# Sliding-window attention into a squared-ReLU MoE layer: first V loaded by token halves, products with V in pairs, column sums spread by copies, and a plan with other costs

## The chip, the core and the metric

One core of one Trainium2 chip. The kernel is a program for five instruction streams (TensorE, ScalarE, VectorE, GpSimd, SyncE; in the profile PE, ACT, DVE, POOL and SP). The metric is the time of one execution on the device in microseconds. A profile is one further execution, recorded instruction by instruction; its span runs from the first to the last instruction.

## What is computed

q, k and v are [8 batches, 8 heads, 576 tokens, 64] in float32. Each token attends to the tokens at most 32 places away; the result, 4608 tokens of 512 numbers, goes through two matrices with a squared ReLU between them.

```python
scores = scale * np.matmul(q, k.transpose(0, 1, 3, 2))
mask = np.abs(pos[:, None] - pos[None, :]) <= window      # window = 32
attn = softmax(np.where(mask, scores, -1e9))
x = (attn @ v).transpose(0, 2, 1, 3).reshape(B * S, H * D)  # [4608, 512]
r = np.maximum(x @ w_in, 0.0)                              # w_in [512, 2048]
out = (s * (r * r) + b) @ w_out                            # w_out [2048, 512]
```

Since `b` is one number, `b @ w_out` is `b` times the column sums of w_out. The kernel computes `s * ((r * r) @ w_out) + b * colsum`.

## The kernel before

**Tasks and a plan.** The kernel writes no instruction directly. It adds tasks to a graph with `add` (L95): a stream, one or more instructions, an estimated cost in ns, the resources that it reads and writes, and a key (a due time; the smaller goes first). `plan` (L126) simulates the streams and the DMA queue with these costs, and each time takes the task that can start first, by key where several can. `emit` (L234) writes each stream in the planned order, with semaphore waits for what comes from other streams. So each engine's order is fixed when the kernel is built; an engine whose next instruction waits stands still, whatever lies behind it. The order of tasks in the program sets who reads and writes a buffer before whom. SP's loads have keys below -100 and go in program order.

**Batches.** Batches 0 and 1 are treated by pairs of heads (`load_pair`, `turn_pair`, `pair_scores`): k and q of a pair are loaded (256 KB each, 512 tokens), cast to bf16 (L691), transposed on PE (L704), copied out (L709 for q on ACT, L710 for k on DVE), multiplied (L943) and put through the exponential (L986). The last 64 tokens come separately (`load_rest`, `turn_rest`, `last_scores`). The products with V are made in units of 128 tokens, five to a batch (`av_part`, L868): half of the 64-row products, a wait, then the other half; then `finish` takes the reciprocal of the row sums (L892), multiplies (L894, DVE), transposes (L901, PE) and copies into XT (L909, ACT). XT is the input of the MoE layer. Later batches go through DMA transposes and `unit`, in which a unit's products with V share a task with the next unit's scores, which then lie between the two halves.

**V of batch 0.** `load_rows` (L595) loads 512 tokens in two DMAs, four heads each; partition p holds tokens 4p to 4p+3, all 128 partitions. One cast for each half of the heads goes to VN (L602). `place_v` (L613) brings the tokens into the right partitions by products with a shifted identity (L620, 24 of them), and the results are copied from PSUM into VB (L629, L630). The last 64 tokens come by `load_tail` and `place_tail`.

**The MoE layer.** `s1` makes one block's hidden values: products with w_in (L1123), ReLU (L1130, ACT), square (L1132, DVE). `s2` multiplies 128 tokens by w_out (L1141) and `put` writes them out (L1157, DVE, then a DMA). The first 512 tokens are cut into blocks of 224, 128 and 160; their products with w_out are made by `early` (L1172) two rows of 128 of w_out at a time as these arrive, into four PSUM banks (both halves of O and of AVN). The first block needs units 0 and 1 of batch 0. `FIRST` lists the order in which the quarters of w_in are used by the three blocks; an entry with `None` lets the attention of batch 1 go one step on.

**Weights.** `load_weights` (L542) loads w_in and w_out in 16 pieces of 512 KB through eight staging buffers and casts each (L556, all on POOL). SP's order after the pairs of batch 0 is `ORDER0`: the two row loads of V, the rest of q and k, the tail of V, then the four quarters of w_in. Then comes `ORDER1`: pairs of batch 1, w_out, V and rest of batch 1.

**Column sums.** `colsum` (L1180) sums w_out by 64 products with ones in 32-column groups (L1182), copies four blocks to a block diagonal (L1186), spreads them over all partitions by one float32 product (L1189) and multiplies by b into CVEC (L1191), which `put` adds.

Of the kernel before, what the change touches and what calls it, by code (L numbers as in the profile page):

```python
# [25 lines left out]
K0 = ("dve", "dve", "dve", "dve")  # L26
Q0 = ("act", "pool", "pool", "pool")
RUN = 4
ORDER0 = (("r", 0), ("r", 1), ("e", 0), ("v", 0), ("w", 0), ("w", 1), ("w", 2), ("w", 3))
ROWE = ("pool", "dve")  # L30
WINE = ("pool", "pool", "pool", "pool")
TURNKEY = -17.5
TURN = (None, 0)
FIRST = ((0, 0), (0, 1), (1, 0), (1, 1), (2, 0), (0, 2), (2, 1), (1, 2), (2, 2), (0, 3), (1, 3), (2, 3), TURN, TURN, TURN, TURN)
WOUTE = (("pool", "pool"),) * 4
TAIL = ("act", "dve")
HOST = (("k", 3), ("q", 0))
HELD = (2200.0, 1500.0, 1500.0, 1500.0)
OPEN = -24.4
REST = ("pool", "pool")  # L40
ORDER1 = (("p", 0), ("p", 1), ("w", 0), ("w", 1), ("p", 2), ("p", 3), ("w", 2), ("w", 3), ("v", 0), ("v", 1), ("e", 0), ("v", 2), ("v", 3), ("v", 4))
SWITCH = 215.0
XTS = 4000.0
# [7 lines left out]
SLACK = (1000.0, 2000.0, 3000.0, 3000.0)  # L51
PACEV = ((-1,-1,0,0,1),(0,0,1,1,2),(0,0,1,1,2))
EV0 = ("dve", "act", "dve", "act", "dve")
BANK1 = ("SC", "W", "SC", "AVN", "AVN")
EV1 = ("pool", "pool", "pool", "pool", "pool")
EV2 = ("dve",) * 5
# [3 lines left out]
TURN_DVE = ()  # L60
# [5 lines left out]
class _Task:  # L66
    __slots__ = ("n", "stream", "fns", "cost", "lat", "key", "deps", "users", "left",
                 "ready", "start", "fin", "dma", "sem", "seq", "val", "used", "snap", "slack", "after", "next", "half", "mark")

    def __init__(self, n, stream, fns, cost, lat, key, dma, slack, after):  # L70
# [10 lines left out]
class _Graph:  # L81
# [4 lines left out]
    LAT = {"pe": 260.0, "act": 130.0, "dve": 110.0, "pool": 150.0, "sp": 60.0}  # L86
    MARGIN = 250.0
# [7 lines left out]
    def add(self, stream, fns, cost, reads=(), writes=(), key=0.0, accum=False, dma=None, waits=(),  # L95
            lat=None, slack=0.0):
# [3 lines left out]
        t = _Task(len(self.tasks), stream, fns, cost, self.LAT[stream] if lat is None else lat, key,  # L100
                  dma, slack, after)
# [4 lines left out]
        for r in reads:  # L106
            assert r in self.writer, r
            t.deps.add(self.writer[r])
        for w in writes:
# [16 lines left out]
    def plan(self):  # L126

        free = {s: 600.0 for s in self.STREAMS}
# [7 lines left out]
        order = []  # L136
        rings, clock, room = {"sp": [], "act": []}, [0.0], {}
# [37 lines left out]
        def release(t):  # L175
            for u in t.users:
                u.left -= 1
                if u.stream == "pe" and t.stream == "pe":
                    r = t.fin
                elif t.dma is not None:  # L180
                    r = t.fin + 100.0 + u.slack
                elif u.stream == t.stream:
                    r = t.fin + 60.0
                else:
                    r = t.fin + t.lat + (self.MARGIN if u.stream == "pe" else 0.0)
# [4 lines left out]
        while len(order) < len(self.tasks):  # L190
# [19 lines left out]
            t.start = st  # L210
            free[t.stream] = t.fin = st + t.cost
# [114 lines left out]
def bass_sliding_window_symmetric__then__act_starrelu_kernel(  # L326
# [23 lines left out]
    with ExitStack() as es:  # L350
# [146 lines left out]
        even, block = OUTS[NOUT - 2][:, 0:128], OUTS[NOUT - 1][:, :]  # L497
        done = [g.tasks[-1]]
        add("pool", lambda e: e.memset(even, 1.0 / 32), 150, writes=[("OUTS", NOUT - 2)], key=-95.0, waits=done)
        add("pool", lambda e: e.memset(block, 0.0), 500, writes=[("OUTS", NOUT - 1)], key=-95.0, waits=done)  # L500
# [41 lines left out]
        def load_weights(which, i, x, key, eng):  # L542
# [6 lines left out]
            else:  # L549
# [7 lines left out]
                {"act": 1040.0, "dve": 690.0, "pool": 1100.0}[eng], reads=[("STG", si)], writes=[("W" + which, i, x)],  # L557
                key=key + 150.0, slack=100.0, lat=HELD[i] if which == "out" else None)

# [643 lines left out]
        for m, i in FIRST:  # L1203
# [3 lines left out]
            for ft in range(4 * i, 4 * i + 4, group(m)):  # L1207
                s1(m, ft)
# [265 lines left out]
```

## Time and profile before

| | us |
|---|---|
| median of 3 runs (313.73 to 314.08) | 313.94 |
| span of the profiled execution | 310.6 |
| DVE busy, of the span | 191.8 |
| POOL busy, of the span | 106.8 |
| first product with V (L868) | starts at 14.80 |
| first MoE product (L1123) | starts at 20.20 |
| last piece of w_out cast (L556) | 43.39 to 44.43 |
| first MoE product of the fourth block | starts at 60.00 |
| DMA traffic | 56.09 MB in 100,054 packets |

The page gives busy time, share of the span and number of instructions for each engine; busy time of PE is modelled from the starts of its products. Its second part cuts the span into 40 slices of 7.8 us; a digit is the busy share in tenths. The chain of waits is followed back from the last instruction to whatever released it. A line of the order of time gives start, duration, engine, line, operation, output<-inputs, shapes and count, and in brackets how long the engine had been idle and what ended that.

### The profile page before, as it was taken

What the parts mean: (1) busy time and instruction counts of PE and PEld (TensorE: products, weight loads), DVE (VectorE), ACT (ScalarE), POOL (GpSimd) and SP (SyncE); (2) the same over time, 40 slices, a digit from 0 to 9 for tenths busy, and PEclk for the clock granted to TensorE, in tenths of its full rate; (3) what the DMA queues carried; (4) which work ended last, traced back from release to release, by engine and by line L of the source; (5) the groups of instructions that cost most, each with busy time, mean ns of one, the idle gap of its engine ahead of it and who ended that gap; (6) DMA issues with size and microseconds to landing.
All of it is one profiled execution on the core that took longest, in us unless ns stands there. A gap on an engine that the chain in (4) does not pass through costs nothing.

```text
span 310.6 us, 7883 instructions
## 1 busy us (share of the span) xinstructions
PE 295.3 (95%) x3305; PEld 160.3 (52%) x3348; DVE 191.8 (62%) x372; ACT 142.3 (46%) x224; POOL 106.8 (34%) x125
## 2 busy tenths in 40 slices
PE   7789999999999999999999999999999999999996
PEld 3469754577654454454444444444444444444444
DVE  4675587776677796886379658866655543333312
ACT  4757445256536673763156326635444333333300
POOL 6364786752526366261435331615000000000000
PEclk9999999999999999999999999999999999999999
DMA  7999999998997998899799799978211111000122
GB/s 223 333 384 372 371 268 235 245 168 271 247 192 210 282 184 192 287 145 154 215 291 151 139 262 281 141 146 203 80 53 53 51 46 36 34 34 35 37 96 77
DMA packets 100054, 56.09 MB, mean 181 GB/s; under 512 B 72048, under 2 KB 91248, under 8 KB 100016
## 3 DMA queue, kind: packets, MB, share of 16 engines
q1 hardware_dynamic: 100016, 55.56, 75.3%
q8 instruction: 27, 0.44, 0.6%
q14 instruction: 11, 0.09, 0.1%
HBM read 36.70 MB, written 9.44 MB: 149 GB/s over the span
## 4 chain that ended last, share of the span: by engine, by line
PE 78%; DMA 12%; SPq 3%; issue 2%; POOL 2%; DVE 2%; ACT 0%; POOLq 0%
PE o L1141 35%; PE w L1123 32%; DMA stg<-in_moe_w_out_dram 5%; PE avn L868 4%; DMA stg<-in_moe_w_in_dram 3%; DMA stg<-in_k_dram 3%; PE sc L810 2%; PE avn L1172 2%; DMA stg<-in_v_dram 1%; DVE gt L1132 1%; SPq L666 1%; PE o L1172 1%; POOL wout L556 1%; SPq L677 1%; PE avn L901 1%
## 5 line engine op out<-in xcount | busy, mean ns | idle before, releaser
L1123 PE MATMUL w<-xt,win 128*128 128x512 bf16 (+4 forms) x750 | 138.2, 325 | 2.9 <-ACT r L1130 1.6
L1130 ACT ACTIVATE r<-w 128x512 bf16<-128x512 f32 (+2 forms) x148 | 86.7, 586 | 100.1 <-PE w L1123 84.9
L1132 DVE TENSOR_TENSOR gt<-r 128x512 bf16<-128x512 bf16 (+2 forms) x148 | 87.1, 601 | 69.2 <-ACT r L1130 68.5
L1141 PE MATMUL o<-wout,gt 128*128 128x512 bf16 (+1 forms) x508 | 120.6, 372 | 2.4 <-issue 1.6
L1123 PEld LDWEIGHTS w<-xt,win 128*128 128x128 bf16 x768 | 68.1, 98 | 52.9 <-ACT r L1130 1.2
L1141 PEld LDWEIGHTS o<-wout,gt 128*128 128x128 bf16 x528 | 50.5, 98 | 55.1 <-DVE gt L1132 0.7
L759 POOL CAST nat<-stg 128x1024 bf16<-128x1024 f32 (+1 forms) x36 | 41.1, 1140 | 51.2 <-DMA stg<-in_q_dram 38.2
L776 POOL COPY kt<-ktr 128x512 bf16<-128x512 bf16 (+1 forms) x30 | 30.8, 1028 | 36.0 <-DMA ktr<-nat 34.5
L838 ACT ACTIVATE ex<-sc 128x1024 bf16<-128x1024 f32 (+1 forms) x28 | 28.7, 1023 | 24.4 <-PE avn L868 23.3
L1157 DVE SCALAR_TENSOR_TENSOR outs<-o,sb,cvec 128x512 f32<-128x512 f32 (+1 forms) x35 | 25.5, 732 | 18.9 <-PE o L1141 18.7
L894 DVE TENSOR_TENSOR xn<-avn,rec 128x512 bf16<-128x512 f32 (+1 forms) x31 | 21.4, 690 | 0.9
L842 DVE TENSOR_TENSOR ex<-ex,mask 128x1024 bf16<-128x1024 bf16 (+1 forms) x28 | 19.8, 708 | 1.2 <-ACT ex L838 0.5
L868 PE MATMUL avn<-vb,ex 64*64 64x65 bf16 x944 | 19.9, 197 | 0.3
L868 PEld LDWEIGHTS avn<-vb,ex 64*64 64x64 bf16 x944 | 12.9, 106 | 13.2 <-issue 5.5
L590 DVE CAST vb<-vst 128x512 bf16<-128x512 f32 (+1 forms) x28 | 12.3, 445 | 1.1 <-DMA vst<-in_v_dram 1.1
L892 DVE RECIPROCAL rec<-avn 128x8 f32<-128x8 f32 (+1 forms) x31 | 6.3, 202 | 8.7 <-PE avn L868 8.7
L810 PE MATMUL sc<-qt,kt 64*64 64x128 bf16 x432 | 11.3, 216 | 0.0
L909 ACT COPY xt<-avn 128x512 bf16<-128x512 bf16 (+2 forms) x14 | 7.1, 517 | 9.0 <-PE avn L901 9.0
L556 POOL CAST wout<-stg 128x1024 bf16<-128x1024 f32 x8 | 8.7, 1087 | 5.9 <-DMA stg<-in_moe_w_out_dram 5.7
L556 POOL CAST win<-stg 128x1024 bf16<-128x1024 f32 x8 | 8.4, 1055 | 3.3 <-DMA stg<-in_moe_w_in_dram 3.2
L1172 PE MATMUL o<-wout,gt 128*128 128x512 bf16 x28 | 8.2, 379 | 0.7 <-POOL wout L556 0.5
L986 ACT ACTIVATE ex<-sc 128x1024 bf16<-128x1024 f32 (+2 forms) x7 | 6.2, 902 | 5.0 <-PE sc L943 5.0
(118 smaller groups left out, 140.5 us busy)
## 6 DMA issues: line engine op xcount, KB each, us to landing
out_dram<-outs SPq DMA_DIRECT2D x35, 256.0 KB, 2.5
vst<-in_v_dram SPq DMA_DIRECT2D x28, 256.0 KB, 6.1
stg<-in_k_dram SPq DMA_DIRECT2D x6, 1024.0 KB, 10.4
stg<-in_q_dram SPq DMA_DIRECT2D x6, 1024.0 KB, 5.8
stg<-in_moe_w_in_dram SPq DMA_DIRECT2D x8, 512.0 KB, 8.8
stg<-in_moe_w_out_dram SPq DMA_DIRECT2D x8, 512.0 KB, 7.2
stg<-in_q_dram SPq DMA_DIRECT2D x8, 256.0 KB, 5.2
stg<-in_k_dram SPq DMA_DIRECT2D x8, 256.0 KB, 5.4
```

Of the source, the lines that this page charges most:

```text
L556: add(eng, (lambda e: e.copy(dst, stg)) if eng == "act" else (lambda e: e.tensor_copy(dst, stg)), {"act": 1040.0, "dve": 690.0, "pool": 11 ...
L759: add(eng, lambda e, x=x: e.tensor_copy(nat[0:top, 1024 * x:1024 * x + 1024].rearrange("p (i h d) -> p h i d", h=H, i=2), stg[0:top, :].re ...
L776: add("pool", lambda e, c=c, w=w: e.tensor_copy(KT[slot][:, :, c:c + w].rearrange("p a (s i) -> p a s i", i=4), KTR[slot][:, :, :, c // 4: ...
L838: add("act", lambda e, dst=flat_dst, src=flat_src: e.activation(dst, src, AF.Exp, bias=0.0, scale=0.125), 190 + 0.833 * 512 * len(hs), rea ...
L842: add("dve", lambda e, flat=flat, mask=mask: e.tensor_tensor(flat, flat, mask, ALU.mult), 130 + 0.53 * 512 * len(hs), reads=[("E", ei, hp, ...
L868: return [lambda e: e.matmul(av[64 * x:64 * x + 64, h, 0:D + 1], lhsT=buf[64 * g:64 * g + 64, h % 2, h // 2, c:c + 64], rhs=VB[64 * g:64 * ...
L894: add("dve", lambda e: e.tensor_tensor(XN[xi][0:p1, :].rearrange("p (a c) -> p a c", a=H), av[0:p1, :, 0:D], REC[ri][0:p1, :].rearrange("p ...
L1123: add("pe", [lambda e, g=g, kc=kc: e.matmul(wt[:, g, :], lhsT=WIN_BF[:, kc, (f0 + g) * 128:(f0 + g + 1) * 128], rhs=XT[:, kc, t0 % XR:t0 % ...
L1130: add("act", lambda e: e.activation(rt, wt, AF.Relu, bias=0.0, scale=1.0), 190 + 0.833 * ng * nt, reads=[("W", wb)], writes=[("R1", rb)], ...
L1132: add("dve", lambda e: e.tensor_tensor(GT[gs][:, f0:f0 + ng, g0:g0 + nt], rt, rt, ALU.mult), 130 + 0.53 * ng * nt, reads=[("R1", rb)], wri ...
L1141: add("pe", [lambda e, fc=fc: e.matmul(O[:, ob, 0:cn], lhsT=GT[gs][:, fc, g0:g0 + 128], rhs=WOUT_BF[:, fc, c0:c0 + cn], start=(fc == 0), s ...
L1157: add("dve", lambda e: e.scalar_tensor_tensor(OUTS[us][:, 0:cn], bank, SB128[:, 0:1], CVEC[:, c0:c0 + cn], ALU.mult, ALU.add), 200 + 1.07 ...
```

## The change

- *V by token halves.* `load_rows(y)` now loads all heads of 256 tokens into 64 partitions (0 to 63, then 64 to 127). Each half is cast in two pieces of heads, all four on POOL. The first of the two loads is issued ahead of the fourth pair of q and k. `place_rows` places two units with 16 products for both pairs in all, into AVN; the second pair waits for the first products with V. 
- *Order of the loads.* The second row load follows the pairs, then the first quarter of w_in, then the rest of q and k, the second quarter, the tail of V, the other two. In batch 1 pair 3 comes before pair 2, and the rest of q and k behind the last of w_out.
- *Products with V in pairs.* `joint` makes one task of several units: all first halves, one wait, all second halves. Batch 0 has the groups (0, 1), (2), (3, 4), batch 1 has (0, 1), (2, 3), and its last unit joins the first scores of batch 2.
- *Column sums.* They go into W instead of AVN, after the first hidden values in the program; the float32 product and its two zeroed buffers go. One scaling by b, then 16 copies of 32x128 on DVE.
- *Engines.* Copies and casts have an engine each (`COPYQ`, `COPYK`, `XTE`, `K1`, `Q1` and others); of eight w_out casts six go to DVE, one to ACT, one to POOL, and the last quarter of w_in to DVE. The turns of batch 1 use W and the two O banks (`TURN1`), its scores O and SC (`SCORE1`).
- *The plan.* Costs of the tasks are new numbers, the delay from one stream to another is a table by both streams, a change of the PE's tile shape costs 92 ns in the plan, and a DVE task marked "two" and a POOL task are not planned side by side. A task on another engine that reads a PSUM bank waits for its other readers.

```diff
-ORDER0 = (("r", 0), ("r", 1), ("e", 0), ("v", 0), ("w", 0), ("w", 1), ("w", 2), ("w", 3))
+ORDER0 = (('r', 1), ('w', 0), ('e', 0), ('w', 1), ('v', 0), ('w', 2), ('w', 3))
-WINE = ("pool", "pool", "pool", "pool")
+WINE = ('pool', 'pool', 'pool', 'dve')
-WOUTE = (("pool", "pool"),) * 4
+WOUTE = (('dve', 'dve'), ('pool', 'dve'), ('dve', 'dve'), ('dve', 'act'))
+VROWS = 3
+TURN1 = (0, 1, 0, 1, 2, 3, 0, 0, 3)
+SCORE1 = ('O', 'SC', 'SC', 'SC')
...
-    LAT = {"pe": 260.0, "act": 130.0, "dve": 110.0, "pool": 150.0, "sp": 60.0}
+    LAT = {"pe": {"act": 210.0, "dve": 210.0, "pool": 210.0, "sp": 210.0},
+           "act": {"pe": 55.0, "act": 0.0, "dve": 35.0, "pool": 35.0, "sp": 40.0},
...
+            t.start, t.fin = st, st + t.cost
+            if t.stream == "pe":
+                t.fin += self.TURNED if (t.form or "full") != shape else 0.0
+                shape = t.form or "full"
+            elif t.form == "two" or (t.stream == "pool" and t.dma is None):
+                mine, other = ("dve", "pool") if t.stream == "dve" else ("pool", "dve")
+                if st < pair[other]:
+                    t.fin = max(t.fin, pair[other] + t.cost - 130.0)
+                pair[mine] = t.fin
...
         def load_rows(y, load_key):
-            dst = VST[:, 0:RUN, :, :].rearrange("p u h d -> p (u h d)")[:, 1024 * y:1024 * y + 1024]
+            p0 = 64 * y
+            dst = VST[p0:p0 + 64, 0:RUN, :, :].rearrange("p u h d -> p (u h d)")
             add("sp", lambda e: e.dma_start(
-                dst.rearrange("p (h c) -> p h c", h=4),
-                v[0, 4 * y:4 * y + 4, 0:128 * RUN, :].rearrange("h (p i) d -> p h (i d)", i=RUN)),
+                dst.rearrange("p (h c) -> p h c", h=H),
+                v[0, :, 256 * y:256 * y + 256, :].rearrange("h (p i) d -> p h (i d)", i=RUN)),
                 600.0, writes=[("VS", y)], key=load_key, dma=("l", 32, 46.0))
...
+        def joint(b, us, key, waits=()):
+            parts = [av_part(b, u) for u in us]
+            ahead = [f for p in parts for f in p[0][0]]
+            t = add("pe", ahead + [None] + [f for p in parts for f in p[0][1]], 303.0 * len(parts) + (130.0 if len(parts) < 2 else 20.0), form="64",
+                    reads=[r for p in parts for r in p[1]], writes=[r for p in parts for r in p[2]], key=key,
+                    slack=1500.0, waits=waits)
+            t.mark = len(ahead) - 1
+            for u in us:
+                land["av", b, u] = t
+                finish(b, u, key + 0.001 * u)
...
             for pr in range(NPAIR):
-                for name in "qk":
+                if pr == VROWS:
+                    load_rows(0, nxt())
+                for name in FIRSTQK[0][pr]:
                     load_pair(0, name, pr, nxt())
...
-            place_v()
-            turn_rest(0, -23.9, banks)
-            place_tail()
+            place_rows((0, 1), -26.3, [land["scores", 0, PLACED]] if PLACED < NPAIR else [])
+            joint(0, (0, 1), -25.0)
+            place_rows((2, 3), -24.7, [land["av", 0, 0]])
+            joint(0, (2,), -20.5, [land["xt", 1]])
+            yield 0
+            turn_rest(0, -20.4, banks)
+            place_tail([])
             last_scores(0)
-            first_units()
+            joint(0, (3, 4), -20.2)
...
-            add("dve", [lambda e, x=x: e.tensor_copy(block[32 * x:32 * x + 32, 128 * x:128 * x + 128],
-                                                     AVN[32 * x:32 * x + 32, 1, 0:128]) for x in range(4)],
-                800, reads=[("AVN", 1)], writes=[("OUTS", NOUT - 1)], key=-12.0)
-            add("pe", lambda e: e.matmul(AVN[:, 1, :], lhsT=even, rhs=block, start=True, stop=True),
-                950, reads=[("OUTS", NOUT - 2), ("OUTS", NOUT - 1)], writes=[("AVN", 1)], key=-12.0)
-            add("dve", lambda e: e.tensor_scalar(CVEC[:, :], AVN[:, 1, :], SB128[:, 1:2], None, ALU.mult),
-                680, reads=[("AVN", 1), ("SB128", 1)], writes=[("CVEC", x) for x in (0, 1)], key=P2[0])
+            some = OUTS[NOUT - 1][:, 0:128]
+            add("dve", lambda e: e.tensor_scalar(some, W[:, 1, 0:128], SB128[:, 1:2], None, ALU.mult),
+                250, reads=[("W", 1), ("SB128", 1)], writes=[("OUTS", NOUT - 1)], key=-12.0)
+            for y in range(4):
+                for x in range(4):
+                    to, part = CVEC[32 * y:32 * y + 32, 128 * x:128 * x + 128], some[32 * x:32 * x + 32, :]
+                    eng = SPREAD[y]
+                    add(eng, (lambda e, to=to, part=part: e.copy(to, part)) if eng == "act" else
+                        (lambda e, to=to, part=part: e.tensor_copy(to, part)), {"act": 300, "dve": 200}[eng],
+                        reads=[("OUTS", NOUT - 1)], writes=[("CVEC", x // 2, y)], key=P2[0] + 0.5)
```

More of the change, by code (lines that the diff above doesn't have):

```diff
@@ L108, in add @@
             t.deps.add(self.writer[r])
+            if r[0] in self.BANKS and not isinstance(r, str):
+                t.deps.update(x for x in self.readers.get(r, ()) if x.stream != stream)
         for w in writes:
@@ L136, in plan @@
         order = []
+        shape, pair = "full", {"dve": 0.0, "pool": 0.0}
         rings, clock, room = {"sp": [], "act": []}, [0.0], {}
@@ new lines, in place_rows @@
+            add("pe", [lambda e, i=i, u=u: e.matmul(
+                AVN[:, u % 2, :].rearrange("p (h c) -> p h c", c=64),
+                lhsT=grid[32 * u:32 * u + 32, RUN - 1 - i:RUN - 1 - i + 128], rhs=VN[32 * u:32 * u + 32, :, i, :],
+                start=(i == 0), stop=(i == RUN - 1), skip_group_check=True) for i in range(RUN) for u in us],
+                60.0 + 110.0 * H, form="row", reads=[("VN", us[0] // 2, z) for z in (0, 1)] + ["PICK"],
+                writes=[("AVN", u % 2) for u in us], key=key, slack=300.0, waits=waits)
```

228 lines of the change are left out of this document (113 added, 115 removed).

## The prediction

> **What bounds it.** I read the page's shares and slices first, then three stretches, then the chain of waits, then the order of time of PE.
>
> ```profile
> PE 295.3 (95%) x3305; PEld 160.3 (52%) x3348; DVE 191.8 (62%) x372; ACT 142.3 (46%) x224; POOL 106.8 (34%) x125
> PE   7789999999999999999999999999999999999996
> DVE  4675587776677796886379658866655543333312
> DMA  7999999998997998899799799978211111000122
> GB/s 223 333 384 372 371 268 235 245 168 271 247 192 210 282 184 192 287 145 154 215 291 151 139 262 281 141 146 203 80 53 53 51 46 36 34 34 35 37 96 77
> ```
>
> ```profile
> 0.00:20.20 20.20, 15.25 (x277) 8.05 (x277) 11.83 (x34) 11.73 (x19) 10.49 (x26) 1.00 0.95 303
> 20.20:60.00 39.80, 37.82 (x569) 26.96 (x564) 27.88 (x55) 19.79 (x35) 28.63 (x38) 1.00 1.09 313
> 60.00:310.60 250.60, 242.25 (x2472) 125.25 (x2509) 152.05 (x284) 110.80 (x170) 67.72 (x63) 1.00 0.69 150
> ```
>
> The stretches give length, then busy time of PE, PEld, DVE, ACT, POOL, the granted clock, DMA share and GB/s. PE stands still 4.95 us before 20.2 us (its first MoE product), 1.98 us from there to 60 us, and 8.35 us in the other 250 us, some 3 of which follow the last product. So from 20 us on PE is the bound, and the clock, 1.00 throughout, plays no part. After 60 us the diff changes planned costs and engines but no work of PE: little is to be won there. What can move lies in the first 60 us, where DMA is full:
>
> ```profile
> 10.00 4.62 DMA stg<-in_v_dram
> 15.27 9.92 DMA stg<-in_moe_w_in_dram
> 26.31 7.23 DMA stg<-in_moe_w_out_dram
> 34.66 7.22 DMA stg<-in_moe_w_out_dram
> 44.48 1.08 PE avn L1182 x64
> 48.08 0.86 PE avn L1189 x2
> ```
>
> The chain (start, length, what) hangs on loads up to 44.5 us, v, then w_in, then w_out, and on PE after that. Whatever is put into the DMA stream before 43 us pushes all that comes behind it.
>
> **The change, term by term** (against the 310.6 us of the profiled execution; the median of 313.94 is 3.36 more, and I add that at the end).
>
> 1. *Column sums.* The float32 product L1189 goes.
>
> ```profile
> 47.92 1.02 PE L1189 MATMUL avn<-outs 128*128 128x512 f32 x2
> 48.87 0.20 PEld L943 LDWEIGHTS sc<-qt,kt 64*64 64x64 bf16 x12 [0.76 <-ACT qt L709]
> L1186 DVE COPY outs<-avn x4: 269/286/298, 46.5 to 47.4; 32x128 f32<-32x128 f32 x4
> ```
>
> From its start to the next instruction 0.95 us pass on a full PE: **-0.95**. The 64 small products before it stay. On DVE four copies of 0.286 and one L1191 of 0.75 (1.9 us) become one scaling (0.25, bounded by 0.21, the reciprocal of 8 columns, and 0.75) and 16 copies of at most 0.286: 4.8 us. The 2.9 us more lie on DVE, whose results only the first output sums (58.1 us) need. I put nothing for it: DVE stands still 11.9 us between 20 and 60. Without that cover it costs up to 2.9.
>
> 2. *Products with V in pairs.* Each unit alone waits between its two halves:
>
> ```profile
> 15.19 0.20 PEld L868 LDWEIGHTS o<-vb,ex 64*64 64x64 bf16 x12 [0.18 <-PE o L868]
> 16.59 0.21 PEld L868 LDWEIGHTS sc<-vb,ex 64*64 64x64 bf16 x16 [0.19 <-PE sc L868]
> ```
>
> Batches 0 and 1 have ten such units. Afterwards there are three groups in batch 0 and two in batch 1, whose last unit joins the scores of batch 2: five waits fewer, 5 x 0.19: **-0.95**. Each group also has a change from 128-row to 64-row products and back. The trace has no row for that alone; PE's gaps there are 0.1 to 0.3 us over the plain product. Five changes fewer are worth between 0 and 1.0: **-0.4**, nearer the lower end since transposes follow anyway. A pair ends later than its first unit did, and its normalisations (0.21 + 0.69 each on DVE) follow one another; that is in term 4.
>
> 3. *Order and engines.* A w_out cast goes from POOL (1.04) to DVE (0.70, the row of the V cast L602 of the same shape), six of eight; two w_in casts likewise; copies of k and q are spread. PE's 1.98 us of standing still between 20 and 60 us are what a better order can win at most, and they hold waits on a w_out cast at 32.28 and 44.48 us (about 0.5 each). Against it: the turns of batch 1 now also use the O banks, so two of the four early output sums start only after the last q and k of batch 1, loaded behind w_out, while before they began at 32.28 us. The products into the AVN banks (16 x 0.433 = 6.9 us), the rest of w_in's and the turns cover that. Bounds -2.0 and +1.0: **-1.2**.
>
> 4. *The start.* SP's queue now issues the first V rows ahead of the fourth pair of k and q, and w_in's first quarter ahead of the remaining rows of q and k. A row load was 512 packets of 1 KB on 128 partitions; now each goes to 64 partitions. The packet records have 46 ns for such a packet: 32 x 46 = 1.47 us. For 64 partitions there is no row. The nearest is the 16-partition loads of L751, landing after 52 us: 156 ns, and
>
> ```profile
> 49.00:52.00 3.00, 2.95 (x56) 1.63 (x54) 2.07 (x5) 1.72 (x2) 1.50 (x2) 1.00 1.10 323
> 52.00:53.00 1.00, 1.00 (x7) 0.47 (x5) 0.64 (x1) 1.00 (x3) 0.87 (x3) 1.00 1.21 113
> ```
>
> the stream falls from 323 to 113 GB/s with the engines full. So a row load costs between 1.47 and 5.0 us; 64 partitions lie nearer to 128 than to 16, and I take 69 ns: 2.2 us, +0.75 each.
>
> The Trainium skill ("SBUF — State Buffer", Door 1: The DMA port swizzle) says that partitions 0 to 63 reach only half of the 16 ports, measured at 196 against 328 GB/s, so that 64 partitions are hardly faster than 32. By its ratio a row load would take 2.5 us by estimate, +1.0 each. The 16-partition rows agree in kind; no row here has 64.
>
> Then the path to the first MoE product: the last of pair 3 lands at 9.84 + 1.47 + 0.75 = 12.1; cast 0.62, turn 0.4, copy 0.69, scores 0.4, exponential 1.02 and some 0.3 of handing over: the first pair of units starts at 15.5 (14.80 before for one unit). Its products take 1.3, two normalisations 1.85, turn 0.4, copy 0.8: 19.9 us against 20.20. So V by halves wins nothing there, but units 3 and 4, the last scores and the tail, some 2.4 us of PE's work done by then before, are still to do. Without the slower packets it starts at 19.1 and 1.5 us are behind. Parts of it fill waits later; the packing is bounded by -0.9 (only the earlier start counts) and +1.5, taken as +0.75, and the late pair 3 adds 0.75: **+1.5**. The second row load's +0.75 delays all of w_in and w_out but stays hidden behind the work now waiting at PE. New waits: the rows of units 2 and 3 stand on PE behind the first pair, so ACT's two evictions (0.59 each) come between copies of XT; 0.3 of the handing over is theirs.
>
> Sum: -0.95 - 0.95 - 0.4 - 1.2 + 1.5 = **-2.0**: a span of 308.6, a median of **312.0 us**.
>
> **Rivals.**
> *B, the start costs nothing:* packets to 64 partitions run at 46 ns and what was put off fills PE's waits. For it: DMA engines take 46 ns in every full 1 KB stretch before 11 us. Against: PE's work done by 20.2 us. Terms 1 and 2, -2.3, and all of the 2.0: -4.3, **309.6**.
> *C, the V halves hold up the DMA stream (slower):* at 92 ns or more for a packet the stream is 64 x 46 = 2.9 us late. Pair 3 pays 1.5 of that, packing 0.75, and the other 1.4 come back when w_out and batch 1 land late and PE runs out; the 1.2 of term 3 are lost too: -2.3 + 3.65 = +1.35, **315.3**. It decides from 89 ns on, where 64 x 43 = 2.75 us outweigh 2.3 + 1.2 - 0.75. For it: 303 GB/s in the first 20 us with DMA at 0.95, no room. Against: only 16-partition loads show it. The page named above, taken at half the ports, is this case.
> *D, DVE becomes the bound:* between 30 and 50 us it is busy 6.14 + 8.94 = 15.1 of 20 (two 10-us stretches), and gets six casts (4.2) and 2.9 of copies, less three k casts (some 2.0): 20.2 of 20. Squares of the hidden layer come late, PE waits about 1.8 us: 312.0 + 1.8 = **313.8**, no change. Against: fewer POOL casts beside it; squares that took 0.39 us alone took 0.83 next to one.
>
> **Chances.** Forecast 0.48, B 0.18, C 0.22, D 0.12. A measurement of this kernel tells about 0.2%, 0.63 us, from no change. Faster (below 313.3): nine tenths of the forecast, B, a fifth of D: 0.63. Same: a tenth of the forecast, most of D: 0.13. Slower: C and a little of D: 0.24. The range reaches from just under B, 309.2, to C, 315.3; the forecast's own, by the bounds of terms 2 to 4, is 310.2 to 313.4.
>
> **What would show it.** Right: no L1189; five fewer waits inside L868; the first L1123 within 0.5 us of 20 us; PE still under 2 us between it and 60 us; the steady part of 250 us equally long. The V row packets give term 4: 46 ns speaks for B, 92 for C. DVE without idle time between 30 and 50 us, and L1141 or L1172 waiting for L1132, would be D. It is wrong if the stretch after 60 us gets longer, since I gave the new order there nothing.

## Result: 909 us, 2.9 times the time before

| | us |
|---|---|
| median after (4 runs, 903.36 to 914.35) | 909.46 |
| median before, beside it (4 runs, 313.24 to 314.08) | 313.84 |
| ratio | 2.8985 [2.8909, 2.9062] |
| span of the profiled execution after | 905.0 |

Here and below, medians leave out executions that took over 1.5% longer than the fastest of the same kernel (one each of e9 and e15, two of e17), and the ratios rest on the others.

Neither the forecast of 312.0 us nor any of the rivals holds this. Two lines of the changed kernel's page (busy time by engine, and a DMA queue with its packets, MB and share of the DMA engines' time), then the one DMA queue of this kind on the page of before:

```profile
PE 684.3 (76%) x7900; PEld 438.1 (48%) x7978; DVE 612.0 (68%) x1211; ACT 367.1 (41%) x661; POOL 113.9 (13%) x146
q10 hardware_dynamic: 155072, 47.20, 22.3%
```

```profile
q1 hardware_dynamic: 100016, 55.56, 75.3%
```

PE has 7900 products where 3305 were recorded before, and a second queue, which is not on the page of before, has moved 47 MB. That is mostly more work, not slower work. The seam is in the order of time:

```profile
329.30 0.48 DVE L1193 SCALAR_TENSOR_TENSOR outs<-o,sb,cvec 128x256 f32<-128x256 f32 x1 [1.26 <-PE o L1177]
331.63 0.45 ACTq L1321 DMA_DIRECT2D stg<-in_q_dram  x1
```

At 329.30 us the last output sum is made: the kernel's usual path is over. At 331.63 q is loaded once more, on ACT's queue, by another function. The kernel holds a second, general path: at the end it tests whether the reciprocals of all row sums lie between 2^-60 and 2^60 (the constant `LEAST`), and where one does not, everything is computed again, safely and slowly. Here that takes 573.4 us (from 331.63 to the end of the span, 905.0). Why the test fails is seen at 60 us, in batch 1 (`rec` is the reciprocal that is tested, `xn` the normalised unit, L922 its transposes):

```profile
60.38 0.91 PE L889 MATMUL sc<-vb,ex 64*64 64x65 bf16 x50
61.41 0.21 DVE L913 RECIPROCAL rec<-sc 128x8 f32<-128x8 f32 x1 [0.86 <-PE sc L889]
62.81 0.39 PE L922 MATMUL sc<-ident,xn 128*128 128x128 bf16 x4
63.75 0.21 DVE L913 RECIPROCAL rec<-sc 128x8 f32<-128x8 f32 x1 [0.37 <-ACT xt L930]
```

The products of *both* units of a pair go to bank SC. The first unit is normalised and transposed back into SC at 62.81, and only at 63.75 are the second unit's row sums read there. They are no row sums any more (the trace shows the order, not the values; the first experiments decide). In the code both units even write the same columns of SC, so that the first unit's own sums are already mixed with the second's at 61.41; which of the two spoils the test is not shown. In the diff it is one line, which was not among those I costed: `BANK1 = ("SC", "W", "SC", "AVN", "AVN")` became `('SC', 'SC', 'O', 'AVN', 'AVN')`, while `joint(1, (0, 1), ...)` makes one task of units 0 and 1. The graph orders tasks by the resources that they write; inside one task it sees nothing.

The usual path is slower too: its last sum starts at 329.30 us, against 307.56 before. The windows (length, busy PE, PEld, DVE, ACT, POOL, granted clock, DMA share, GB/s) and two places of its start:

```profile
0.00:20.20 20.20, 12.95 (x109) 5.41 (x109) 7.41 (x24) 7.51 (x10) 6.63 (x19) 0.79 0.95 210
20.20:60.00 39.80, 37.25 (x523) 26.68 (x528) 25.11 (x57) 25.89 (x45) 13.26 (x17) 0.89 0.99 307
```

```profile
20.02 2.14 POOL L630 CAST gt<-vst 64x1024 bf16<-64x1024 f32 x2 [4.43 <-DMA vst<-in_v_dram]
27.32 1.68 PE L1159 MATMUL w<-xt,win 128*128 128x224 bf16 x8
```

The DMA engines are as busy as before (0.95) but move 210 GB/s instead of 303; V's second half is cast at 20 us, the first MoE product starts at 27.32 instead of 20.20, and the clock is 0.79 and 0.89 where it was 1.00. The experiments take these apart: first the bank, then what the usual path loses.

### The profile page after: what moved, and what is told of

Same layout as the page of the kernel before. It is cut to its first block, busy times and chain, and to the rows that moved or that the text cites. A ratio compares the mean times of both kernels' runs of the same rounds, so it can differ in the third digit from the quotient of the medians.

```text
span 905.0 us, 18869 instructions
## 1 busy us (share of the span) xinstructions
PE 684.3 (76%) x7900; PEld 438.1 (48%) x7978; DVE 612.0 (68%) x1211; ACT 367.1 (41%) x661; POOL 113.9 (13%) x146
## 4 chain that ended last, share of the span: by engine, by line
PE 38%; DVE 25%; DMA 19%; ACT 8%; issue 5%; POOL 2%; ACTq 1%; SPq 1%; POOLq 0%; DVEq 0%
PE o L1400 10%; PE o L1177 8%; DMA stg<-in_k_dram 8%; PE w L1388 7%; PE w L1159 7%; DMA stg<-in_q_dram 6%; DVE rec L1368 4%; DVE stg L1360 3%; DVE stg L1358 3%; DVE nat L1324 3%; DVE rec L1362 3%; ACT stg L1366 3%; DMA ktr<-nat 2%; DVE stg L1364 2%; ACT r L1392 2%
## 5 line engine op out<-in xcount | busy, mean ns | idle before, releaser
L1388 PE MATMUL w<-xt,win 128*128 128x128 bf16 x2304 | 159.5, 233 | 11.0 <-ACT xt L1382 9.4
L1388 PEld LDWEIGHTS w<-xt,win 128*128 128x128 bf16 x2304 | 146.4, 105 | 16.7 <-ACT xt L1382 11.2
L1400 PE MATMUL o<-wout,gt 128*128 128x512 bf16 x540 | 123.7, 382 | 33.4 <-DVE rec L1370 23.4
L1392 ACT ACTIVATE r<-w 128x512 bf16<-128x512 f32 x144 | 85.7, 600 | 85.7 <-PE w L1388 67.3
L1324 DVE CAST nat<-stg 128x512 bf16<-128x512 f32 (+1 forms) x152 | 63.6, 421 | 53.7 <-DMA stg<-in_q_dram 18.5
L1400 PEld LDWEIGHTS o<-wout,gt 128*128 128x128 bf16 x576 | 54.1, 98 | 91.3 <-DVE gt L1394 30.3
L1159 PEld LDWEIGHTS w<-xt,win 128*128 128x128 bf16 x768 | 69.2, 99 | 55.5 <-ACT r L1166 1.5
L1394 DVE TENSOR_TENSOR gt<-r 128x512 bf16<-128x512 bf16 x144 | 60.4, 421 | 39.9 <-ACT r L1392 38.1
L1177 PEld LDWEIGHTS o<-wout,gt 128*128 128x128 bf16 x528 | 50.3, 98 | 54.7
L1368 DVE TENSOR_REDUCE rec<-stg 128x4 f32<-128x512 f32 x72 | 49.1, 682 | 19.9 <-ACT stg L1366 18.8
L1364 DVE TENSOR_TENSOR stg<-stg,rec 128x512 f32<-128x512 f32 x72 | 49.6, 689 | 1.6
L1360 DVE TENSOR_TENSOR stg<-stg 128x512 f32<-128x512 f32 x72 | 49.4, 686 | 0.4
```

The source lines that it names most:

```text
L1159: add("pe", [lambda e, g=g, kc=kc: e.matmul(wt[:, g, :], lhsT=WIN_BF[:, kc, (f0 + g) * 128:(f0 + g + 1) * 128], rhs=XT[:, kc, t0 % XR:t0 % ...
L1177: add("pe", [lambda e, fc=fc: e.matmul(O[:, ob, 0:cn], lhsT=GT[gs][:, fc, g0:g0 + 128], rhs=WOUT_BF[:, fc, c0:c0 + cn], start=(fc == 0), s ...
L1324: add("dve", lambda e: e.tensor_copy(NAT[x][0:n, 0:DM], STG[x][0:n, 0:DM]), 500, reads=[("in", x)], writes=[("nat", x)], key=step())
L1360: add("dve", lambda e: e.tensor_tensor(by_pair(SS), by_pair(SS), once[1], ALU.add), 700, reads=["ss", "bias"], writes=["ss"], key=step())
L1368: add("dve", lambda e: e.tensor_reduce(SUM, by_pair(PP), mybir.AxisListType.X, ALU.add), 700, reads=["pp"], writes=["sum"], key=step())
L1388: add("pe", [lambda e, f=f, kc=kc: e.matmul(wt[:, f, :], lhsT=WIN_BF[:, kc, (f0 + f) * 128:(f0 + f) * 128 + 128], rhs=XT[:, kc, x0:x0 + 12 ...
```

## Experiments

Ratios are against the kernel before, run beside each on the same chip; the interval is 95%.

### The bank and the test (e1_bank, e2_apart, e3_fallback)

```diff
e1_bank: the changed kernel
-BANK1 = ('SC', 'SC', 'O', 'AVN', 'AVN')
+BANK1 = ('SC', 'W', 'O', 'AVN', 'AVN')
e2_apart: the changed kernel, both units in SC
-            for us in ((0, 1), (2, 3)):
+            for us in ((0,), (1,), (2, 3)):
e3_fallback: the kernel before
-LEAST = 2.0 ** -60
+LEAST = 2.0 ** 60
```

> The changed kernel with one bank renamed: the second unit of batch 1 has its products with V in W, where it was, instead of in SC beside the first unit. Theory (T1): in one joint task both units write the same bank SC, the first unit's transposes overwrite the second's row sums, the guard on the row sums fails and the whole general path runs behind the usual one; with its own bank the guard holds and only the usual path is left, which ends at 330 us in the trace of the changed kernel: 325 to 340 us. Rival (T2): the guard fails for another reason, for instance what the new orders leave in a bank before an exponential: 890 to 920 us again.

> The changed kernel with the first two units of batch 1 as two tasks again, both still in SC. T1: as tasks they follow one another through the bank, so the guard holds: 325 to 342 us. If SC itself is wrong for the second unit, or T2 holds, 890 to 920 us.

> The kernel before with a guard that always fails (limit 2^60 instead of 2^-60): the price of the general path alone. T1: 314 plus the 575 us that lie behind the usual path in the changed kernel's trace: 870 to 900 us. If the changed kernel's time were lost elsewhere, this would be far from its 909 us.

Measured: 331.09 us, ratio 1.0583 [1.0436, 1.0730]; 332.52 us in one run; 880.25 us. One entry of a table is worth 578 us. With both units still in SC but in tasks of their own it is gone as well, so it is the bank *inside one task*, not the bank. The kernel before, with a test that always fails, takes 568 us more (880.25 in one run, 312.66 beside it): that is the price of the general path. It is 573 in the changed kernel, whose new planning costs hold there too; that they make the difference is not shown.

The 331.09 us of e1_bank is the median of two runs, 3.75 us apart, and its interval is 4.6 us to either side. Differences from e1_bank below are no better known than that.

### What a copy, a cast and a load cost (m1_prices)

A small kernel that computes nothing of the reference: 16 copies on DVE alone, then beside casts on GpSimd, then on ACT beside casts; and loads to 128, 64 and 32 partitions.

> No part of the reference's computation: row loads of V in four layouts one after the other, and 16 copies of 32x128 float32 on DVE alone, on DVE beside casts on POOL, and on ACT beside casts on POOL; the output is zeros. Theory (P): a load to partitions 0 to 63 or 64 to 127 reaches half of the ports, so its 1 KB packets take about 92 ns and more against 46 on 128 partitions, two such loads some 6 us against 3, and 64 partitions in steps of two run at full rate. Rival: packets take 46 ns in all layouts, and the late landing in the changed kernel comes from the queue. Theory (L): DVE's copies from SBUF wait for the end of each POOL cast of 1.04 us: 0.2 us each alone, 0.6 to 1.1 beside casts; on ACT 0.3 either way. Rival: a copy between partition groups takes 0.67 us anyway.

Its order of time (start, length, what):

```profile
3.05 3.69 DVE L71 COPY cvec<-outs 32x128 f32<-32x128 f32 x16
7.87 13.20 DVE L71 COPY cvec<-outs 32x128 f32<-32x128 f32 x16 [1.14 <-POOL dst L80]
7.90 12.16 POOL L83 CAST dst<-src 128x1024 bf16<-128x1024 f32 x11
22.87 4.90 ACT L97 COPY cact<-outs 32x128 f32<-32x128 f32 x16 [1.14 <-POOL dst L87]
```

Sixteen copies take 3.69 us alone, 0.23 from one to the next, and 13.20 beside casts on GpSimd. In the second row the copies differ: eleven lie beside the eleven casts, one to a cast, and take up to 1.10 each (median 1.09), while the one before the casts and the four after them take 0.22. On ACT, with casts beside it, sixteen take 4.90.

The packet records give the loads, two of 512 KB in each layout. To 128 partitions a 1 KB packet takes 46 ns, and the two loads move 283 GB/s over 3.7 us (385 once the queue is full). To partitions 0 to 63 and then 64 to 127 packets take 46 ns in the first microsecond, then 64 to 89 (medians of half microseconds), and the two loads move 206 GB/s over 5.1 us. To 64 partitions in steps of two packets take 46 ns again, and the rate reaches 383 GB/s. The page "SBUF — State Buffer" of the Trainium skill, Door 1: The DMA port swizzle, gives 196 GB/s for partitions 0 to 63: the trace agrees in kind, with 206, but for the first microsecond. "SBUF — State Buffer" of the Trainium skill, Who interferes with whom, says of the port pair that VectorE and GpSimd share that whoever issues first has it for the whole instruction and the other waits, where VectorE works in a mode that uses it. The 1.09 us beside casts of 1.04 agree.

### Where the usual path loses (e4_act, e5_heads, e6_heads_late_act, e7_spread_alone)

In e1_bank PE stands still for 8 us. The order of time there:

```profile
67.51 9.81 DVE L1230 COPY cvec<-outs 32x128 f32<-32x128 f32 x16
69.22 2.14 POOL L780 CAST nat<-stg 128x1024 bf16<-128x1024 f32 x2 [1.43 <-DMA stg<-in_q_dram]
72.83 4.40 POOL L797 COPY kt<-ktr 128x512 bf16<-128x512 bf16 x4
77.69 1.40 DVE L1193 SCALAR_TENSOR_TENSOR outs<-o,sb,cvec 128x512 f32<-128x512 f32 x2
80.47 0.43 PE L889 MATMUL o<-vb,ex 64*64 64x65 bf16 x16 [8.04 <-DVE outs L1193]
```

The 16 copies take 9.81 us beside GpSimd's work (0.21 to 1.09 each); squares and the first output sums are queued behind them on DVE; the sums hold bank O, for which PE waits until 80.47. The windows of the same kernel show a second price, the granted clock behind the busy times:

```profile
72.15:77.00 4.85, 0.27 (x3) 0.00 (x0) 4.75 (x6) 0.00 (x0) 4.55 (x5) 0.99 0.76 135
77.00:80.47 3.47, 0.00 (x1) 0.01 (x2) 3.44 (x7) 0.60 (x1) 0.86 (x2) 0.50 0.50 159
80.47:83.70 3.23, 3.15 (x74) 2.36 (x75) 3.08 (x9) 0.60 (x1) 0.00 (x0) 0.50 0.55 199
```

The gap begins at 72.43 (80.47 less 8.04). Some 4.5 us into it the clock falls to 0.50, and stays there for 3.2 us after work is back. "TensorE: Matmul & The Clock Gate" of the Trainium skill (HAM oscillation) says that a gap of more than about 3.4 us lets the clock fall: this gap agrees.

```diff
e4_act: e1_bank and
-SPREAD = ('dve', 'dve', 'dve', 'dve')
+SPREAD = ('act', 'act', 'act', 'act')
e5_heads: e1_bank and, in load_rows,
-            dst = VST[p0:p0 + 64, 0:RUN, :, :].rearrange("p u h d -> p (u h d)")
+            dst = VST[:, 0:RUN, :, :].rearrange("p u h d -> p (u h d)")[:, 1024 * y:1024 * y + 1024]
...
-                v[0, :, 256 * y:256 * y + 256, :].rearrange("h (p i) d -> p h (i d)", i=RUN)),
+                v[0, 4 * y:4 * y + 4, 0:128 * RUN, :].rearrange("h (p i) d -> p h (i d)", i=RUN)),
... (and one cast for each load in place of two)
e6_heads_late_act: both, and both row loads behind the four pairs
-VROWS = 3
+VROWS = 4
-ORDER0 = (('r', 1), ('w', 0), ('e', 0),
+ORDER0 = (('r', 0), ('r', 1), ('w', 0), ('e', 0),
e7_spread_alone: the kernel before with the column sums by 16 copies on DVE
```

> The kernel with unit 1 of batch 1 in W (331.09 us), and the 16 copies on ACT in place of DVE. Theory L (beside GpSimd's casts the 16 copies take 9.8 us instead of 3.7, the first output sums wait for them, PE stands still for 8.2 us at 72 us): 16 copies of 0.31 us on ACT, 5.0 us, start at the same place and end near 73 us; the gap falls under 2 us and the time by 6 to 8 us, to 323 to 325. Rival R (the early output sums wait because the new order puts w_out's last pieces and batch 1 behind each other, whatever the copies take): the gap stays above 6 us, the time stays above 329.

> The kernel with unit 1 of batch 1 in W (331.09 us), and V's rows loaded as before: four heads in each load, 128 partitions, one cast each; both at the places of the changed order. Theory P (packets to 64 partitions take 82 to 98 ns, V lands late, PE waits and its granted clock falls to 0.5 until 29 us): packets go back to 46 ns, both casts are done before 15 us, the first MoE product starts between 19.5 and 21.5 us instead of 25.9, the clock is 1.00 up to there, and the time falls by 5 to 8 us, to 323 to 326. Rival R (it is the place of the first row load ahead of pair 3, and four weight quarters behind them, that delay the start): the first MoE product still starts after 24 us, the time stays above 328.

> Both edits (copies on ACT, V by four heads over 128 partitions) and both row loads behind the four pairs, as before the change. Theories P and L together, and nothing else wrong: the two gains add, 331.1 - 7 - 7 = 317, and less where the clock stays at 1.00 up to 85 us (another 3 to 5 us): 310 to 317; the rest of the change is then worth between -3 and +4 us against before. If the rest of the order (joint units, engines, delays) costs something itself, it stays above 317.

> The kernel before with the column sums by 16 copies on DVE alone. As predicted (term 1: the float32 product away, the copies hidden under DVE's waits): ratio 0.997, -0.95 us. Theory L (the copies stretch beside GpSimd's casts, and the first output sums wait for them): in the kernel before all w_out casts are on GpSimd, the copies come after the last of them at 44.4 us, so little is lost; -1 to +1 us. If the copies alone brought the 8 us stall, +6 to +9 us.

Measured: 327.12 us (1.0436 [1.0406, 1.0465]); 329.08 (1.0507 [1.0464, 1.0549]); 325.15 (1.0366 [1.0343, 1.0389]); 316.18 (1.0073 [1.0049, 1.0097]). None of the four came out as my theories said; e5 came out as its rival did.

*e4* won 4.0 us, not 6 to 8. The copies on ACT do not stretch, but now ReLU is queued behind them. The order of time of e6, where they are on ACT too:

```profile
65.03 5.00 ACT L1228 COPY cvec<-outs 32x128 f32<-32x128 f32 x16 [1.57 <-DVE outs L1222]
70.05 1.08 ACT L1165 ACTIVATE r<-w 128x512 bf16<-128x512 f32 x2
70.70 4.01 PEld L1158 LDWEIGHTS w<-xt,win 128*128 128x128 bf16 x24 [4.54 <-ACT r L1165]
```

PE waits 4.5 us for the ReLU of 70.05. So the waiting beside GpSimd is about half of what the column sums cost (7.8 to 9.1 us, see below); the other half is that sixteen instructions stand in one block ahead of work that PE needs, on whichever engine.

*e5* has its packets at 46 ns again, and still starts its first MoE product at 25.22 (25.87 in e1) and wins 2.0 us, which the spread of e1 does not tell from nothing. The slow packets are real, and V's casts are done at 14.12, but that alone does not bring the start back: the first products of `place_rows` come only at 15.74 and take 1.89 us, both evictions of a pair follow one another on DVE (1.29 us, for which PE waits 1.39), and the clock is at 0.70 in the first 20 us. *e6* moves the first MoE product to 23.14 and stays at 325.

*e7* says what term 1 as a whole is worth in the kernel before: +2.3 us, where I had put -0.95. Three lines of its order of time:

```profile
56.94 4.85 POOL L755 CAST nat<-stg 128x1024 bf16<-128x1024 f32 x4 [1.39 <-DMA stg<-in_k_dram]
57.30 0.95 DVE L1188 COPY cvec<-outs 32x128 f32<-32x128 f32 x1
60.70 0.40 PE L897 MATMUL sc<-ident,xn 128*128 128x128 bf16 x4 [1.51 <-DVE xn L890]
```

The last copy, beside a cast, takes 0.95 instead of 0.22; masks and the normalisation come late behind it, and PE waits 1.51 for that. Another wait of 1.34 us, at 53.75, is for a copy of k behind four of the copies on DVE.

### Start and column sums put back (e9_old_sums, e10_old_start, e11_old_start_sums, e12_pairs_alone)

```diff
e9_old_sums: e1_bank with the float32 product (in W) in place of the copies
e10_old_start: e1_bank with the start as before
-ORDER0 = (('r', 1), ('w', 0), ('e', 0), ('w', 1), ('v', 0), ('w', 2), ('w', 3))
+ORDER0 = (('r', 0), ('r', 1), ('e', 0), ('v', 0), ('w', 0), ('w', 1), ('w', 2), ('w', 3))
-            place_rows((0, 1), -26.3, [land["scores", 0, PLACED]] if PLACED < NPAIR else [])
...
-            joint(0, (3, 4), -20.2)
+            place_v()
+            turn_rest(0, -23.9, banks)
+            place_tail([])
+            last_scores(0)
+            first_units()
... (and V's loads, the engines of the first casts and copies, as before)
e11_old_start_sums: both
e12_pairs_alone: the kernel before, with joint() and these groups
...
+            joint(0, (0, 1), -25.0)
+            joint(0, (2,), -23.0, [land["xt", 0]])
+            joint(0, (3, 4), -22.0, [land["xt", 2]])
...
+            for us in ((0, 1), (2, 3)):
+                joint(1, us, due(1, us[0]))
```

> The kernel with unit 1 of batch 1 in W (331.09 us), with the column sums spread by the float32 product as before, in bank W, and no copies. Theory L': not the lock alone but any 16 copies ahead of the work that PE waits for cost (on DVE 9.8 us, on ACT 5.0 us with a gap of 4.4 us left): without them no gap of over 2 us is left between 60 and 85 us, the clock stays at 1.00 there, and the time falls below the 327.1 us of the copies on ACT, to 321 to 324. Rival R (the early output sums come late by the order of loads and turns): a gap of 4 us stays near 70 us and the time is 326 or more.

> The kernel with unit 1 of batch 1 in W (331.09 us), with the start as before the change up to the first MoE product: loads and their order, casts and copies, V placed in three groups over AVN, W and SC, the five units of batch 0 one by one. The copies of the column sums stay on DVE. Theory S (the start costs through late V and through the gathering of everything behind the first pair, and the clock of 0.5 that follows an idle PE): first MoE product at 20 to 20.5 us, clock 1.00 until 60 us, time 331.1 - 8 to 10, so 321 to 323, and the gap near 72 us of 8 us stays. Rival: the start is only shifted work, and less than 4 us come back: over 327.

> Both of these: start and column sums as before the change; what is left of the change is the pairs in batch 1 (each in its own banks), the engines, the order of batch 1 and of w_out, and the plan with its new costs. Theory: the two losses are all that the change costs beside the bank, so this stands at the kernel before or below it: 310 to 313.5, ratio 0.99 to 1.00, with PE in the steady part after 100 us as dense as in the trace of e6 (0.35 to 0.6 us lost in 10, against 0.3 to 1.0 before). Rival (the new order of w_out, batch 1 and casts costs by itself): ratio over 1.005.

> The kernel before with products in pairs alone: groups (0, 1), (2), (3, 4) in batch 0 and (0, 1), (2, 3) in batch 1, each unit in a bank of its own. As predicted (term 2): five waits of 0.19 and changes of shape fewer, -1.35 us, ratio 0.996. Rival (the pair ends later than its first unit did, and the first MoE product waits for both normalisations): it starts 0.5 to 1.5 us later than at 20.2 and PE stands still for it: ratio 1.000 to 1.003.

Measured: 322.04 us (1.0286 [1.0241, 1.0331]); 324.24 (1.0320 [1.0282, 1.0358]); 316.44 (1.0101 [1.0057, 1.0144]); 315.03 (1.0052 [1.0029, 1.0075]). e9 came out as its theory said. In e10 the first MoE product starts at 21.55, later than I expected, and the clock is 0.50 from 15.8 to 22.6 us. In the changed order the column sums are worth 9.1 us (from e1 to e9) or 7.8 (from e10 to e11), the start 6.9 (e1 to e10) or 5.6 (e9 to e11); together they win 14.7. So the two add, as far as two runs of e1 can tell. The windows of e11:

```profile
0.00:20.20 20.20, 15.63 (x248) 7.66 (x249) 11.69 (x34) 11.64 (x19) 10.15 (x25) 1.00 0.92 295
20.20:60.00 39.80, 38.10 (x567) 26.68 (x565) 25.05 (x54) 24.53 (x44) 17.19 (x27) 1.00 1.07 314
60.00:90.00 30.00, 29.19 (x428) 20.03 (x429) 23.69 (x44) 13.82 (x21) 15.77 (x18) 1.00 1.02 217
```

PE's busy time in the first 60 us and the clock of 1.00 are those of the kernel before, and the first MoE product starts at 19.92. Still 1.0% is missing, so the rival of that expectation holds: the rest of the change costs some 3 us as well. It is not the clock: this execution, at 1.00 throughout, takes 316.37, about the median of the six. Pairs alone cost 1.6 us instead of winning 1.35.

### What is left (e13 to e18)

```diff
e13_pairs_one: the kernel before, pairs in batch 1 alone
e14_pairs_zero: the kernel before, pairs in batch 0 alone
e15_no_pairs: e11 with the units of batch 1 one by one, in SC, W, SC, AVN, AVN
e16_wout_casts: the kernel before
-WOUTE = (("pool", "pool"),) * 4
+WOUTE = (('dve', 'dve'), ('pool', 'dve'), ('dve', 'dve'), ('dve', 'act'))
e17_old_slack: e11 with HELD, SLACK and XTS as before
e18_old_delays: e17 and the delays between streams as before
```

> The kernel before with pairs (0, 1) and (2, 3) in batch 1 alone, each unit in a bank of its own; the last unit joins the first scores of batch 2. As predicted: two or three waits of 0.19 and two changes of shape fewer, -0.6 to -0.9 us, ratio 0.997 to 0.998. Rival (pairs as such cost, since both normalisations follow one another ahead of the transposes): +0.5 to +1, ratio 1.002 to 1.003.

> The kernel before with groups (0, 1), (2), (3, 4) in batch 0 alone. Theory (the first MoE product waits for both units' normalisations, 0.9 us more on DVE, and PE, which already stands still for 5 us in the first 20, stands longer and may fall to a clock of 0.5): first MoE product 1 to 3 us later than 20.2, ratio 1.003 to 1.006, so this holds the whole loss of the pairs. As predicted: two waits fewer, -0.4 to -0.6, ratio 0.998.

> The kernel with bank, start and column sums put back (316.44 us), and the units of batch 1 one by one in SC, W, SC, AVN, AVN: what is left of the change is the engines, the order of w_out and batch 1, and the plan's costs and delays. Theory (what is left costs because the plan now and then puts a unit ahead of its inputs: 2.2 us at 176 us, waiting for the copies of k behind a DMA transpose): 315.5 to 317.5, with such a stall between 100 and 200 us. Rival (it was batch 1's pairs): back to 313 to 314, ratio within 0.2% of 1.

> The kernel before with the changed engines for the casts of w_out alone: six on DVE, one on GpSimd, one on ACT. As predicted (part of term 3): the two waits on a w_out cast of 0.5 us each shrink, 0 to -1 us, ratio 0.997 to 1.000. Rival D (DVE gets 4.2 us of casts between 30 and 50 us and squares come late): +0.5 to +2 us, ratio 1.002 to 1.006.

> Start, bank and column sums put back (316.44 us), and SLACK, HELD and XTS as before. Theory (with no allowance for the late casts and only 40 ns for a load, the plan puts a unit ahead of its DMA transpose and PE waits, 2.2 us at 176 us): no gap of over 1 us after 100 us, 314 to 315. Rival (the new allowances only move work): 316 to 317, with such a gap.

> The same with the delays between streams as before too (260, 130, 110, 150 and 60 ns by stream, 60 within one, 100 behind a load, the margin of 250 for all of PE's inputs). Theory: the delays, measured or not, matter little once the allowances stand: within 0.5 us of the run with old allowances. Rival (shorter delays let the plan interleave so tightly that any lateness stops PE): 1 to 2 us below it, 313 to 314, and no gap of over 0.6 us after 20 us.

| | us | ratio |
|---|---|---|
| e13_pairs_one | 314.12 | 1.0013 [0.9988, 1.0037] |
| e14_pairs_zero | 314.93 | 1.0044 [1.0020, 1.0067] |
| e15_no_pairs | 318.19 | 1.0161 [1.0113, 1.0209] |
| e16_wout_casts | 314.08 | 1.0011 [0.9990, 1.0032] |
| e17_old_slack | 317.24 | 1.0109 [1.0072, 1.0146] |
| e18_old_delays | 317.85 | 1.0124 [1.0101, 1.0146] |

The loss of the pairs lies in batch 0. The mechanism that I had given for it does not show: e14's first MoE product starts at 19.85, not later. (In the profile of e12 it starts at 22.34, but there PE ran at a clock of 0.50 from 11.7 to 18.6 us.) What e14's profile shows instead is a clock of 0.50 from 19.5 to 22.9 us, a mean of 0.93 between 20.2 and 40 us: 0.07 x 19.8 = 1.4 us of full clock. That is the size of the loss, yet it explains little of it: seven of e14's twelve executions had a mean clock of 0.999 or more, and their median, 314.56, is still 1.2 us above the 313.36 of such executions of the kernel before. So most of the loss seems not to be the clock, and its cause is open. In batch 1 pairs alone can't be told from no change. Nor can the w_out casts. Without the pairs of batch 1 e11 gets some 1.8 us slower, though the intervals overlap.

The stall that I blamed for the rest, in e11:

```profile
176.82 3.41 POOL L825 COPY kt<-ktr 128x512 bf16<-128x512 bf16 x3 [4.13 <-DMA ktr<-nat]
178.02 0.32 PE L917 MATMUL avn<-vb,ex 64*64 64x65 bf16 x16 [2.04 <-POOL kt L825]
```

is real: the plan put a unit on PE ahead of its k, which came by a DMA transpose and a copy. But with the old allowances it stays (2.2 us at 177 us) and the time is no better, and with the old delays too it goes, other waits come (2.4 us at 32 us for w_out), and the time is again no better. What costs the last 3 us is **open**: putting back the pairs of batch 1, the allowances, or the allowances and delays together did not win it, and the w_out casts do not cost it in the kernel before. The other engines, the order of the loads in batch 1, its turns through the O banks and the planned costs of the tasks were not tried by themselves. No version was faster than the kernel before.

## Why the prediction was wrong

- *The step that failed* is in term 2. It priced "five waits fewer" and changes of shape, and took for granted that the units of a group have banks of their own, as units 0 and 1 of batch 1 had before (SC and W). The list of banks in the changed kernel says otherwise. A wait between two tasks was also what kept two users of one bank apart; taking the wait out takes that away too. And the kernel turns such a fault into time: 578 of the 596 us. That units in one task could spoil each other's sums was not among my rivals, though the test and the second path were in the program.
- *Term 2's own size* was wrong in sign: -1.35 forecast, +1.6 [0.9, 2.4] measured alone, +1.4 of it in batch 0; why is open.
- *Term 1*: the float32 product's 0.95 us was read rightly, but the 2.9 us of copies put at nothing were not hidden. DVE's 11.9 us of standing still are a sum over 40 us; the copies come in a block, stretched by GpSimd's casts (0.22 alone, up to 1.09 beside a cast, over my bound of 0.286), ahead of what PE waits for. -0.95 + 2.9 = +1.95 would have been near the +2.3 of e7, though not for the right reason; in the changed order it is 7.8 to 9.1.
- *Term 3*, -1.2: w_out's casts alone +0.3 [-0.3, 1.0]; no part of the 1.2 was seen anywhere.
- *Term 4*, +1.5: the first MoE product came 5.7 us later than before in e1, and the start as a whole cost 5.6 to 6.9 us. The packets took 80 to 112 ns in the changed kernel between 8 and 16 us (medians of 256 packets), not 69, and those of pair 3, which went to 128 partitions, were slowed with them. The last 1 KB packet of batch 0 starts at 16.40 in e1 and at 12.44 in e5, so that the stream ends 4.0 us later with row loads to 64 partitions than with the same loads to 128. I had taken 1.5; the bound from the 16-partition rows (156) would have given 7. The estimate by "SBUF — State Buffer", Door 1, of the Trainium skill was 2.0, nearer but short. Yet putting the packets right (e5) won only 2.0 us of the time; the rest is the order and the clock, not taken apart further.
- *"The clock plays no part"* was true of the trace before and no property of the kernel: after, PE stood still at the start and the clock was 0.50 for most of the time from 8 to 29 us. Nor need the 8.35 us after 60 us all be standing still: the trace of before has 2472 products there against 2509 weight loads, and a product that is missing from the record reads as standing still. The forecast did not rest on that figure.
- *Rivals*: C had the packets right (92 ns) and its stream of 2.9 us late was nearest to the 4.0 measured; its 3.65 for the start stand against 5.6 to 6.9. That it named the right side is no merit: 578 of the 596 us come from elsewhere. B fell. D named DVE, and DVE did come to stand ahead of PE, but through a block of copies and not through its sum of work.

## What to carry to other kernels

When tasks are merged, list the buffers that they write before listing the waits saved: a planner that orders tasks by resources is blind inside one. Where a kernel has a guard with a slow path, "the guard now fires" is the first rival of any change that touches the data under it. Idle time summed over a stretch hides nothing by itself: ask where the new block stands in its engine's queue, and which wait of the bottleneck lies behind it.

## What was not expected of the hardware

- A stretch of partly idle PE is enough for the clock to fall, without a long gap: in e12 the work up to 12 us is that of the kernel before, PE is busy 0.41 to 0.71 of each us from 6 to 11 and never stands still for as long as 0.9 us, and from 11.8 us the clock is 0.50. The first and last of these windows:

```profile
6.00:7.00 1.00, 0.41 (x14) 0.25 (x14) 0.24 (x1) 0.25 (x1) 0.41 (x2) 1.00 0.99 318
12.00:18.40 6.40, 6.40 (x62) 2.71 (x62) 2.91 (x5) 3.93 (x8) 3.05 (x4) 0.50 1.08 323
```

  The kernel before lost clock now and then too: of the 17 runs beside e12 one had a mean clock of 0.984 (its span 313.1 us, against 310.7 to 313.0 of the others).
- Loads to 64 partitions run at full rate in steps of two (46 ns a packet, up to 383 GB/s) and more slowly as one block (64 to 89 ns after the first microsecond in m1_prices, 80 to 112 in the changed kernel).
- Small float32 copies on DVE that take 0.22 us alone take 1.09 beside casts on GpSimd, one copy to a cast, and 0.30 on ACT.
